# Second MoE: expert rests of 129 to 160 rows as one single block and one small block

## The chip, the cores and the metric

The kernel runs on one core of one Trainium2 chip. The metric is device time in microseconds (us) of one execution, the median of several; lower is better. Engines are named as in the profile: PE (TensorE), DVE (VectorE), ACT (ScalarE), POOL (GpSimd) and SP (SyncE, here only an issuer of DMAs).

## The reference, cut to what matters

Three stages run one after the other: a gated linear attention over 4 x 768 tokens with 8 heads of 48, a first MoE in which every token goes through all weights, and a second MoE in which every token goes to one of eight experts. Only the second MoE is changed:

```python
expert_idx = np.argmax(logits, axis=1)          # N = 3072 tokens, E = 8 experts
out = np.zeros((N, D), dtype=np.float32)        # D = 384
for e in range(E):
    mask = expert_idx == e
    h = np.maximum(x[mask] @ w1[e], 0.0)        # 384 x 1024
    out[mask] = gate_w[mask, None] * (h @ w2[e])  # 1024 x 384
```

On the inputs of the reference the eight experts get 1305, 521, 427, 153, 107, 15, 14 and 530 rows; of the first 22 of 24 tiles of 128 tokens they get 1199, 473, 380, 147, 98, 15, 14 and 490.

## The kernel before

**Stages.** Phase 1 computes attention and the first MoE; its instructions are recorded and put in an order by a planner of the kernel's own (all of them have line L368). Phase 2 is the second MoE. Between them, tokens are sorted into blocks of up to 128 rows: `route_early` does it for the first 22 tiles and hands out up to PE = 4 pairs of blocks (256 rows of one expert each); `late_route` does it for all rows that are left, on DVE, while phase 2 is already at work on the early blocks. It makes late pairs (up to PL = 8) of rests over 128 rows (`pairs_of` with `least` 129), single blocks of at most 128 rows, and up to MINI = 5 small blocks of at most MT = 32 rows. Its results are `btab` (expert of each step, and whether it differs from the step before), `mtab` (expert of each small block), `srcrow` (rows to gather), `dstrow` (rows to scatter to) and `slotgate`.

**Steps.** `STEPS` lists the blocks in order: block 0, block 1, then pairs (p) and single blocks (s). Before it is "ppppp" "s" "pppppp" behind the first two, so 14 steps, numbered k = 0 to 13; the blocks of pairs have the numbers 2 to 23, the single block 24. Further single blocks stand as spares and are run only if more are needed, which these inputs don't. Small blocks have no step: `WITH` names the steps beside which they run (5, 7, 9, 11, 12).

**A step** (`moe2`, driven by `phase2`): `load` fetches the expert's two weight matrices (1536 KB each, queues `q1_buf` and `q2_buf`, two sets deep) on SP's queue, with a condition: nothing is moved if the expert is that of the step before. `gather` fetches rows with an indirect DMA on POOL's queue into `xg`, two steps ahead, four buffers. `prep` splits the weights of the next step into a high and a low part: ACT writes `w1s` and `w2h` (L1288, L1297), DVE writes `w1l` and `w2l` (L1292, L1298); a single block needs no `w1l`. `transpose` turns the next step's rows on PE (`pxg`, L1313), ACT and DVE write `xh`, `xl`. `mm1` (L1336) writes `ph` in PSUM, three buffers; ACT takes `hhi` from it (L1340), DVE `hlo` (L1341). `mm2` (L1352) writes `py`, two buffers; ACT scales it to `yo` (L1356) and POOL scatters `yo` to `out` with an indirect DMA (L1358).

**A small block** (`small`) goes through seven stages between the parts of its step and the next one: load of `w1m` (L1371), gather of `xgm` (L1373), load of `w2m` (L1379), transposes `pxm` (L1383) with `xm` on ACT, matmul `phm` (L1390) with `hm` on ACT, transposes `pt` (L1397) with `hT` on DVE, matmul `pym` (L1405) with `part` on ACT, and one matmul `psm` (L1410) with `ym` on ACT. `w1m` and `w2m` have one buffer each, so the load of the next small block's `w1m` waits on SP for this one's `phm`, and `w2m` for `pym`.

**Order.** In phase 2 each engine's instructions are put in a fixed order when the program is built, by a scheduler that estimates times; then each engine, and each of the queues of SP and POOL, works strictly in that order. Every scatter to `out` also waits for the landing of the scatter before it. Two pieces decide which step carries a small block and when its first weights are asked for:

```python
                elif after:
                    load(k + 1)
                    p = prep(*STEPS[k + 1])
                if k in WITH:
                    next(small_now)                  # w2m
                if k + 1 in WITH:
                    small = self.small(pool, mp, pg, WITH.index(k + 1))
                    next(small)                      # w1m, xgm
                next(p, 0)
```

Of the kernel before, what the change touches and what calls it, by code (L numbers as in the profile page):

```python
# [15 lines left out]
ALU = mybir.AluOpType  # L16
# [11 lines left out]
E = 8  # L28
# [6 lines left out]

TE, PE, PL, SG = 22, 4, 8, E
KE, KP = 2 * PE, 2 * (PE + PL)
NBLK = KP + SG  # L40
MT, MINI = 32, 5

SPARE = 7


def steps(order):

    out, p, s = [(0, 1), (1, 1)], 2, KP
    for c in order:
        out.append((p, 2) if c == "p" else (s, 1))  # L50
        p, s = (p + 2, s) if c == "p" else (p, s + 1)
    assert (p, s) == (KP, NBLK - SPARE)
    return out + [(i, 1) for i in range(s, NBLK)]


STEPS = steps("ppppp" "s" "pppppp")

WITH = 5, 7, 9, 11, 12
NE, NS = 1 + PE, len(STEPS)

TESTS = 6 * NU + 6 + NTILE
# [46 lines left out]
def bc(ap, axis, n):  # L108

    a = ap.unsqueeze(axis)  # L110
    shape = list(a.shape)
    shape[axis] = n
    return a.to_broadcast(shape)
# [269 lines left out]
class Prog:  # L383
# [65 lines left out]
    def consts2(self):  # L449
# [7 lines left out]
        q.gpsimd.memset(self.order, -1.0)  # L457
        for k, (i, n) in enumerate(STEPS[NE:]):
            q.gpsimd.memset(self.order[:, k, 2 - n:3 - n], float((i - KE) // 2 if n == 2 else i - KP))
# [495 lines left out]
    def pairs_of(self, new, cnt, T, n, least, name):  # L955

        v = self.q.vector

        k256 = self.k128[:, 1 + (least == 256):min(T + 1, NTILE):2]
        gt, num, tk = new([E, k256.shape[1]], name + "gt"), new([E], name + "n"), new([E], name + "t")  # L960
        v.tensor_tensor(gt, bc(cnt, 2, k256.shape[1]), bc(k256, 1, E), op=ALU.is_ge if least == 256 else ALU.is_gt)
        v.tensor_reduce(num, gt, axis=AX.X, op=ALU.add)
        st, end = self.sums(new, num, name)
        v.tensor_scalar_min(tk, st, float(n))
        v.scalar_tensor_tensor(tk, end, float(n), tk, op0=ALU.min, op1=ALU.subtract)
        return num, st, end, tk
# [190 lines left out]
    def late_route(self, pool, pg):  # L1157

        v, t = self.q.vector, self.q.tensor
        T, N = NTILE, NBLK + MINI - KE  # L1160

        def new(shape, name, dt=F32):
            return pool.tile([128] + shape, dt, name=name)
        late = slice(TE, T)
        lg, mx = self.choose(new, self.ss[:, late], self.lg[:, late], self.oh[:, :, late])
        rank, cnt = self.ranks(new, pg.tile([128, 2, E, T], F32, tag="rt", bufs=1, name="within"), T)

        taken, slot = new([E], "taken256"), new([E, T], "slot1")

        def take(n):  # L1170
            v.tensor_scalar_mul(taken, n, 256.0)
            v.tensor_sub(cnt, cnt, taken)
            v.tensor_sub(rank, rank, bc(taken, 2, T))
        take(self.taken)
        left, base, ends = new([E, T], "left"), new([2, E], "base"), new([2, E], "ends")
        v.tensor_scalar(left, rank, 0.0, None, op0=ALU.is_ge)
        _, st, end, tk = self.pairs_of(new, cnt, T, PL, 129, "mid")
        v.tensor_copy(ends[:, 0], end)
        take(tk)

        v.tensor_add(base[:, 0], st, tk)
        v.tensor_scalar(base[:, 0], base[:, 0], 256.0, 1.0, op0=ALU.mult, op1=ALU.add)
        v.tensor_add(slot, rank, bc(base[:, 0], 2, T))
        v.scalar_tensor_tensor(slot, rank, 0.0, slot, op0=ALU.is_lt, op1=ALU.mult)

        gt, nb = new([E, T], "cgt"), new([E], "nblocks")
        v.tensor_tensor(gt, bc(cnt, 2, T), bc(self.k128, 1, E), op=ALU.is_gt)
        v.tensor_reduce(nb, gt, axis=AX.X, op=ALU.add)

        few, bm = new([E], "few"), new([MINI, E], "bem")  # L1190
        v.tensor_scalar(few, cnt, float(MT), None, op0=ALU.is_le)
        v.tensor_mul(few, few, nb)
        stm, endm = self.sums(new, few, "few")
        v.scalar_tensor_tensor(few, stm, float(MINI), few, op0=ALU.is_lt, op1=ALU.mult)
        v.tensor_sub(nb, nb, few)
        v.memset(endm[:, E - 1:], 4096.0)
        v.tensor_tensor(bm, bc(self.blk[:, :MINI], 2, E), bc(endm, 1, MINI), op=ALU.is_ge)
        em = new([MINI], "emini")
        v.tensor_reduce(em, bm, axis=AX.X, op=ALU.add)
        v.tensor_copy(self.mtab, em)  # L1200
        st, end = self.sums(new, nb, "late")
        v.tensor_copy(ends[:, 1], end)

        v.tensor_scalar(self.flags[:, 1:2], end[:, E - 1:], float(SG - SPARE), None, op0=ALU.is_gt)

        v.memset(ends[:, :, E - 1:], 4096.0)
        be, m = new([NS - NE, 2, E], "beq"), NS - NE
        v.tensor_tensor(be, bc(self.order, 3, E), bc(ends, 1, m), op=ALU.is_ge)
        v.tensor_reduce(self.bef[:, NE:], be, axis=AX.XY, op=ALU.add)
        v.tensor_copy(self.tab[:, 0, NE:], self.bef[:, NE:])  # L1210
        v.tensor_tensor(self.tab[:, 1, NE:], self.bef[:, NE:], self.bef[:, NE - 1:NS - 1], op=ALU.not_equal)

        v.tensor_scalar(base[:, 1], st, 128.0, 1.0 + 128 * (KP - KE), op0=ALU.mult, op1=ALU.add)

        v.tensor_scalar(stm, stm, 128.0, 1.0 + 128 * (NBLK - KE), op0=ALU.mult, op1=ALU.add)
        v.tensor_sub(stm, stm, base[:, 1])
        v.tensor_mul(stm, stm, few)
        v.tensor_add(base[:, 1], base[:, 1], stm)
        s2 = new([E, T], "slot2")
        v.tensor_add(s2, rank, bc(base[:, 1], 2, T))  # L1220
        v.scalar_tensor_tensor(s2, rank, 0.0, s2, op0=ALU.is_ge, op1=ALU.mult)
        v.tensor_add(slot, slot, s2)
        v.tensor_mul(slot, slot, left)
        self.gate(new, lg, mx, self.gates[:, late])
        yield
        at, val = self.slots(new, slot, T, N)
        ps = pg.tile([128, 5 * N], F32, tag="rt", bufs=1, name="slots")
        for t0 in range(0, T, 6):
            pos = pool.tile([128, 6, 128], BF16, tag="ohpos", bufs=2, name=f"ohpos{t0}")
            v.tensor_tensor(pos, bc(self.pos128, 1, 6), bc(at[:, t0:t0 + 6], 2, 128), op=ALU.is_equal)  # L1230
            self.place(ps, pos, val, t0)
        tok, e0 = new([N], "tok"), new([2, N], "empty")
        self.join(tok, self.gate_of[:, KE:], ps)
        v.tensor_scalar(e0[:, 0], tok, 1.0, 0.0, op0=ALU.subtract, op1=ALU.max)
        v.tensor_copy(self.src[:, KE:], e0[:, 0])
        v.tensor_scalar(e0[:, 1], tok, 0.0, 4097.0, op0=ALU.is_equal, op1=ALU.mult)
        v.scalar_tensor_tensor(e0[:, 1], tok, -1.0, e0[:, 1], op0=ALU.add, op1=ALU.add)
        v.tensor_copy(self.dst, e0[:, 1])
        self.flag(self.cp, pg)
        yield  # L1240
# [177 lines left out]
    def phase2(self):  # L1418
        tc, nc = self.tc, self.nc
        with ExitStack() as ctx:  # L1420
# [12 lines left out]
            late = self.late_route(rp, pg)  # L1433
            gather(*STEPS[1])
            load(0)
            first = prep(*STEPS[0])
            for _ in range(2):
                next(first)
            last = NS - SPARE
            few = iter(())  # L1440
            for k, (i, n) in enumerate(STEPS[:last]):
                if k + 2 < last:
                    gather(*STEPS[k + 2])
                p, after = iter(()), k + 1 < last
# [4 lines left out]
# [4 lines that stand above are left out]
                    next(small_now)  # L1453
                if k + 1 in WITH:

                    small = self.small(pool, mp, pg, WITH.index(k + 1))
                    next(small)
# [6 lines left out]
                for _ in few:  # L1464
                    pass
                if k in WITH:
                    few = small_now
                    next(few)
                if k + 1 in WITH:
                    small_now = small  # L1470
# [79 lines left out]
    def last_blocks(self):  # L1550

        nc = self.nc
        t, v, s, k0, i0 = nc.tensor, nc.vector, nc.scalar, NS - SPARE, STEPS[NS - SPARE][0]
        with self.tc.tile_pool(name="lb", bufs=1) as p, self.tc.tile_pool(name="lbg", bufs=1, space=PSUM) as pg, \
                self.tc.For_i(0, SPARE, 1) as k:

# [230 lines left out]
```

## Time and profile before

| | us |
|---|---|
| Median of 3 runs | 777.73 |
| Lowest and highest run | 777.09, 779.57 |
| The profiled execution | 777.83 |
| Its span in the trace | 775.9 |
| Phase 2, from its first `mm1` on PE to the end of the last `mm2` | 514.2 to 768.0 |

The profiled execution took 1.9 us more than the span of its trace. Times in the trace count from the span's start. In the trace the duration of one matmul overlaps with that of the next, so the length of a stretch of work on PE is taken from the start of its first matmul to the start of the next stretch. A step of phase 2 starts on PE with its first `ph` matmul and ends with the first of the next step.

### The profile page before, as it was taken

The page shows a single profiled execution, that of the slowest core. Times are in us where ns is not written, and L with a number is a line of the kernel's source. Part 1 is how long each engine was busy: PE and PEld are TensorE (multiplying, and loading weights), DVE is VectorE, ACT ScalarE, POOL GpSimd, SP SyncE. Part 2 cuts the span into 40 slices and gives each one's busy share as a digit, 9 for nine tenths or more (in the row PEclk, how much of TensorE's full clock was granted, in tenths as well). Part 3 has the DMA queues.
Part 4 walks back from the last instruction along what each step waited for, and adds up shares of the span by engine and source line. Part 5 has one row for each costly group of instructions (what it writes and reads, how often), then busy time and mean ns, then how long its engine had stood idle before and what let it go on. Part 6 is the DMA issues. An engine that isn't in the chain of part 4 may idle for free. (4 is left out here: it accounts for less than half of the span.)

```text
span 775.9 us, 18425 instructions
## 1 busy us (share of the span) xinstructions
PE 719.6 (93%) x7318; PEld 657.1 (85%) x7318; DVE 607.1 (78%) x1211; ACT 441.5 (57%) x1007; POOL 104.6 (13%) x156
## 2 busy tenths in 40 slices
PE   0568989999999999999999999999999999999995
PEld 0447679899899989888998988989989898999985
DVE  8999799999999999999999722869986455546420
ACT  8997485656667555757455442167535466544521
POOL 6301000000000000000000000022122223324211
PEclk9987899999999999999999999999999999999999
DMA  8608062635345380834516240051058775691500
GB/s 330 263 21 197 1 174 69 139 131 137 106 105 119 91 209 13 197 99 119 137 37 140 60 86 22 13 233 42 22 236 335 283 299 213 210 368 49 186 22 26
DMA packets 28753, 107.42 MB, mean 138 GB/s; under 512 B 5061, under 2 KB 8180, under 8 KB 25569
## 3 DMA queue, kind: packets, MB, share of 16 engines
q1 hardware_dynamic: 20432, 77.55, 33.5%
q0 software_dynamic: 7952, 28.21, 11.3%
q8 instruction: 59, 0.97, 0.5%
q10 hardware_dynamic: 272, 0.39, 0.1%
q14 instruction: 38, 0.30, 0.1%
HBM read 96.35 MB, written 10.62 MB: 138 GB/s over the span
## 5 line engine op out<-in xcount | busy, mean ns | idle before, releaser
L368 PE MATMUL ph<-xhi,w 128*128 128x256 f32 x864 | 134.0, 291 | 0.9 <-ACT xhi L368 0.9
L368 PEld LDWEIGHTS ph<-xhi,w 128*128 128x128 f32 x864 | 114.3, 191 | 8.3 <-issue 4.7
L1298 DVE TENSOR_TENSOR w2l<-queue_q_buf,w2h 128x768 fp32r<-128x768 f32 x52 | 47.9, 954 | 39.1 <-ACT w2h L1297 39.0
L1336 PE MATMUL ph<-xh,w1s 128*128 128x256 f32 x264 | 77.0, 292 | 0.0
L368 PE MATMUL ph<-xlo,w 128*128 128x256 f32 x432 | 75.3, 283 | 0.4 <-DVE xlo L368 0.4
L1336 PE MATMUL ph<-xh,w1l 128*128 128x256 f32 x264 | 74.6, 283 | 0.0
L1336 PE MATMUL ph<-xl,w1s 128*128 128x256 f32 x264 | 74.6, 283 | 0.0
L1352 PE MATMUL py<-w2h,hlo 128*128 128x384 f32 x200 | 67.9, 340 | 1.8 <-DVE hlo L1341 1.8
L1352 PE MATMUL py<-w2h,hhi 128*128 128x384 f32 x200 | 69.1, 345 | 0.0
L1352 PE MATMUL py<-w2l,hhi 128*128 128x384 f32 x200 | 67.6, 338 | 0.0
L368 PEld LDWEIGHTS ph<-xlo,w 128*128 128x128 f32 x432 | 62.0, 191 | 0.6 <-DVE xlo L368 0.6
L368 POOL DMA_DIRECT2D v<-v x24 | 12.9, 538 | 365.4 <-PE py L368 364.5
L1341 DVE SCALAR_TENSOR_TENSOR hlo<-ph,hhi 128x512 fp32r<-128x512 f32 x50 | 34.3, 688 | 30.0 <-ACT hhi L1340 30.0
L1340 ACT ACTIVATE hhi<-ph 128x512 fp32r<-128x512 f32 x50 | 29.9, 598 | 49.0 <-PE ph L1336 48.8
L368 PE MATMUL pa<-S 112*128 112x128 f32 x384 | 51.7, 279 | 2.2 <-DVE at L368 1.7
L1336 PEld LDWEIGHTS ph<-xh,w1s 128*128 128x128 f32 x264 | 50.5, 191 | 3.8 <-issue 3.1
L368 PEld LDWEIGHTS pa<-S 112*128 112x128 f32 x384 | 48.2, 193 | 4.5 <-DVE at L368 2.9
L1297 ACT CAST w2h<-queue_q_buf 128x768 fp32r x52 | 40.8, 833 | 18.1 <-PE py L1352 16.7
L1336 PEld LDWEIGHTS ph<-xh,w1l 128*128 128x128 f32 x264 | 50.5, 191 | 0.5
L1336 PEld LDWEIGHTS ph<-xl,w1s 128*128 128x128 f32 x264 | 50.5, 191 | 0.0
L368 DVE TENSOR_TENSOR sa<-X 128x384 f32<-128x384 f32 x84 | 46.5, 554 | 0.7
L1292 DVE TENSOR_TENSOR w1l<-queue_q_buf,w1s 128x1536 fp32r<-128x1536 f32 x22 | 38.6, 1759 | 9.3 <-PE ph L1336 7.4
(399 smaller groups left out, 1809.1 us busy)
## 6 DMA issues: line engine op xcount, KB each, us to landing
queue_q_buf<-w SPq DMA_DIRECT2D x26, 1536.0 KB
S<-QK SPq DMA_DIRECT2D x46, 289.1 KB
X<-a SPq DMA_DIRECT2D x11, 768.0 KB
QKr<-qk SPq DMA_DIRECT2D x11, 768.0 KB
w1m<-w SPq DMA_DIRECT2D x5, 1536.0 KB
w2m<-w SPq DMA_DIRECT2D x5, 1536.0 KB
v<-v POOLq DMA_DIRECT2D x24, 224.0 KB, 3.6
r<-w POOLq DMA_DIRECT2D x12, 384.0 KB, 8.4
```

Source lines behind the costliest of these rows:

```text
L368: getattr(getattr(self.nc, c[0]), c[1])(*c[2], **c[3])
L1292: v.tensor_sub(wl[k], av.rearrange("p (a b) -> p a b", b=FF2)[:, :, c], w1[k].bitcast(F32))
L1297: s.copy(hi, b[:, c])
L1298: v.tensor_sub(lo, bv[:, c], hi.bitcast(F32))
L1336: t.matmul(ph[:, f], a, b, start=o == 0, stop=o == len(ops) - 1)
L1340: s.activation(hi, ph, AF.Relu).ins,
L1341: v.scalar_tensor_tensor(lo, ph, 0.0, hi.bitcast(F32), op0=ALU.max, op1=ALU.subtract).ins]
L1352: t.matmul(py, a[:, f, r], c[:, k % 4], start=o == 0, stop=o == 3 * KF - 1)
```

## The change

Rests of 129 to 160 rows (128 + MT) are no longer a pair of two blocks. They go as one single block of 128 rows and one small block with the other 1 to 32. On the reference's inputs this concerns one expert, number 3 with 153 rows. There are then 7 late pairs, 2 single blocks and 6 small blocks, in 14 steps as before: block 0, block 1, "ppppppsppspp". The blocks of pairs have the numbers 2 to 21, the single blocks 22 and 23. `WITH` becomes 5, 6, 7, 9, 10, 12. By experts, steps 6 to 13 were 1, 4 (single), 1, 2, 2, 3, 7, 7, and are now 1, 1, 3 (single), 2, 2, 4 (single), 7, 7.

```diff
-TE, PE, PL, SG = 22, 4, 8, E
+TE, PE, PL, SG = 22, 4, 7, E + 2
-MT, MINI = 32, 5
-
-SPARE = 7
+MT, MINI = 32, 6
+
+SPARE = 8
-STEPS = steps("ppppp" "s" "pppppp")
-
-WITH = 5, 7, 9, 11, 12
+STEPS = steps("ppppppsppspp")
+
+WITH = 5, 6, 7, 9, 10, 12
...
-        v.tensor_tensor(gt, bc(cnt, 2, k256.shape[1]), bc(k256, 1, E), op=ALU.is_ge if least == 256 else ALU.is_gt)
+        v.scalar_tensor_tensor(gt, bc(cnt, 2, k256.shape[1]), float(least % 128), bc(k256, 1, E), op0=ALU.subtract,
+                               op1=ALU.is_ge)
...
-        _, st, end, tk = self.pairs_of(new, cnt, T, PL, 129, "mid")
+        _, st, end, tk = self.pairs_of(new, cnt, T, PL, 128 + MT + 1, "mid")
...
-        v.tensor_scalar(few, cnt, float(MT), None, op0=ALU.is_le)
-        v.tensor_mul(few, few, nb)
+        v.scalar_tensor_tensor(few, nb, -128.0, cnt, op0=ALU.mult, op1=ALU.add)
+        v.tensor_scalar(few, few, float(MT - 128), None, op0=ALU.is_le)
+        v.scalar_tensor_tensor(few, nb, 1.0, few, op0=ALU.min, op1=ALU.mult)
...
+        v.tensor_scalar_mul(nb, nb, 128.0)
         v.tensor_sub(stm, stm, base[:, 1])
+        v.tensor_sub(stm, stm, nb)
         v.tensor_mul(stm, stm, few)
-        v.tensor_add(base[:, 1], base[:, 1], stm)
-        s2 = new([E, T], "slot2")
-        v.tensor_add(s2, rank, bc(base[:, 1], 2, T))
+        s2, s3 = new([E, T], "slot2"), new([E, T], "slot3")
+        v.tensor_tensor(s3, rank, bc(nb, 2, T), op=ALU.is_ge)
+        v.tensor_mul(s3, s3, bc(stm, 2, T))
+        v.tensor_add(s3, s3, bc(base[:, 1], 2, T))
+        v.tensor_add(s2, s3, rank)
```

The order of phase 1 stays as it was, but for one more memset on POOL near the start. In phase 2 the scheduler gives other orders. Three places are shown, with the line numbers of each program (L1267 to L1413 of before are L1273 to L1419 of the changed program).

SP's queue, from a small block's second weights to the weights of a single block. Before, this is block 24 (`w2m0` belongs to the small block of step 5):

```order
L1379 DMA w2m0_8052<-w22 128x3072
L1251 TENSOR_LOAD btab_95
L1255 TENSOR_LOAD btab_95
L1257 ISA
L1260 COMPARE_AND_BRANCH
L1261 ISA
L1261 DMA queue_6708_q1_buf<-w21 128x3072
L1262 ISA
L1262 DMA queue_6709_q2_buf<-w22 128x3072
```

In the changed program, the same for block 22 (`w2m1` and `w1m2` belong to the small blocks of steps 6 and 7):

```order
L1385 DMA w2m1_8360<-w22 128x3072
L1374 TENSOR_LOAD mtab_103
L1377 ISA
L1377 DMA w1m2_8365<-w21 128x3072
L1257 TENSOR_LOAD btab_95
L1261 TENSOR_LOAD btab_95
L1263 ISA
L1266 COMPARE_AND_BRANCH
L1267 ISA
L1267 DMA queue_6709_q1_buf<-w21 128x3072
L1268 ISA
L1268 DMA queue_6710_q2_buf<-w22 128x3072
```

The single block's weights now stand behind `w1m2`, the first weights of the next small block. The same holds for block 23, behind `w1m4`.

ACT, where the single block's `w1s` is copied from the queue. Before, this stands in the first matmuls of step 5 (blocks 8 and 9):

```order
L1340 ACTIVATE hhi8_0_1_8122<-ph8_0_1_8103 128x512
L1385 COPY xm0_8130<-pxm0_8126 128x96
L1274 ISA
L1288 COPY w1s24_0_8369<-queue_6708_q1_buf 128x1536
L1340 ACTIVATE hhi8_1_0_8153<-ph8_1_0_8134 128x512
L1340 ACTIVATE hhi8_1_1_8176<-ph8_1_1_8157 128x512
L1288 ISA
L1288 COPY w1s24_1_8370<-queue_6708_q1_buf 128x1536
```

In the changed program it stands in the second matmuls of step 6 (blocks 10 and 11), followed by `w2h` and the first `hhi` of step 7:

```order
L1362 ACTIVATE yo10_8562<-py10_0_8537,slotgate_102 128x384
L1294 COPY w1s22_0_8686<-queue_6709_q1_buf 128x1536
L1294 COPY w1s22_1_8687<-queue_6709_q1_buf 128x1536
L1362 ACTIVATE yo11_8599<-py10_1_8574,slotgate_102 128x384
L1413 COPY part1_8613<-pym1_8604 128x384
...
L1303 COPY w2h22_0_8688<-queue_6710_q2_buf 128x768
L1303 COPY w2h22_1_8690<-queue_6710_q2_buf 128x768
L1346 ACTIVATE hhi12_0_0_8712<-ph12_0_0_8693 128x512
```

The copies of the single block's weights moved from two steps ahead of its step to a step and a half ahead, and now have `yo11`, `part1` and `hhi12` behind them. Further on in step 7, the copy `w1s14_0` of the pair after it stands ahead of `hhi12_1_0`. Steps 9 and 10 have the same order with blocks 14, 23, 16 and 18 in place of 10, 22, 12 and 14.

POOL's queue, at the end of step 3 (blocks 4 and 5), where the gathers for step 5 (`xg8`, `xg9`) wait for `srcrow` of `late_route`. Before:

```order
L1358 DMA out<-yo3_7483,srcrow_97 3072x384
L1267 DMA xg8_7490<-x1d_113,srcrow_97 128x384
L1267 DMA xg9_7494<-x1d_113,srcrow_97 128x384
L1267 DMA xg10_7743<-x1d_113,srcrow_97 128x384
L1267 DMA xg11_7747<-x1d_113,srcrow_97 128x384
L1358 DMA out<-yo4_7704,srcrow_97 3072x384
L1358 DMA out<-yo5_7736,srcrow_97 3072x384
L1373 DMA xgm0_7799<-x1d_113,srcrow_97 128x384
```

In the changed program:

```order
L1364 DMA out<-yo3_7490,srcrow_97 3072x384
L1364 DMA out<-yo4_7711,srcrow_97 3072x384
L1364 DMA out<-yo5_7743,srcrow_97 3072x384
L1273 DMA xg8_7497<-x1d_113,srcrow_97 128x384
L1273 DMA xg9_7501<-x1d_113,srcrow_97 128x384
L1273 DMA xg10_7750<-x1d_113,srcrow_97 128x384
L1273 DMA xg11_7754<-x1d_113,srcrow_97 128x384
L1379 DMA xgm0_7806<-x1d_113,srcrow_97 128x384
```

Two scatters went ahead of the gathers, and the small block's gather no longer stands behind them. On DVE in the same place, the last `hlo` of step 3 (`hlo4_1_0`, `hlo4_1_1`) stood behind the large operations of `late_route` (`ohval`, `ohpos`), and now stands ahead of them; `xl6` and one `w2l8` now stand ahead of `srcrow`.

## Rows read from the trace of the kernel before

**Rows 1.** The page: the span, and PE's busy time.
```profile
span 775.9 us, 18425 instructions
PE 719.6 (93%) x7318; PEld 657.1 (85%) x7318; DVE 607.1 (78%) x1211; ACT 441.5 (57%) x1007; POOL 104.6 (13%) x156
```

**Rows 2.** Who PE waited for, 512 to 776 us.
```profile
PE py L1352 <- DVE hlo L1341: 1.8, 1, 1.8
PE pxm L1383 <- DMA xgm<-x1d,srcrow: 0.8, 1, 0.8
```

**Rows 3.** Stretches: steps 3, 4, 7, 9, 10, and a part of step 3.
```profile
core 0: us, PE busy (x) PEld busy (x) DVE busy (x) ACT busy (x) POOL busy (x), PEclk, DMA share, GB/s
552.93:576.66 23.73, 21.93 (x156) 21.07 (x155) 22.88 (x45) 10.08 (x14) 5.13 (x4) 0.93 0.28 110
576.66:594.05 17.39, 17.39 (x126) 17.39 (x126) 9.80 (x13) 9.98 (x14) 5.08 (x5) 1.00 1.01 412
634.38:646.80 12.42, 12.42 (x108) 11.35 (x108) 6.21 (x9) 8.70 (x13) 5.04 (x5) 1.00 0.45 162
666.76:688.20 21.44, 21.44 (x173) 19.09 (x172) 11.93 (x14) 11.77 (x19) 6.59 (x5) 1.00 0.69 250
688.20:706.56 18.36, 18.36 (x133) 18.09 (x129) 9.87 (x12) 9.66 (x15) 5.06 (x5) 1.00 0.62 246
...
572.00:576.00 4.00, 4.00 (x17) 4.00 (x16) 3.27 (x10) 0.36 (x1) 2.80 (x3) 0.58 1.00 421
```

**Rows 4.** PE in order of time, step 5: start, length, operation.
```profile
604.13 1.50 PE L1390 MATMUL phm<-w1m,xm 128*32 128x256 f32 x24
605.56 0.87 PE L1313 MATMUL pxg<-ident,xg 128*128 128x128 f32 x6
...
610.44 0.38 PE L1397 MATMUL pt<-ident,hm 128*128 128x128 f32 x2
...
614.94 1.50 PE L1405 MATMUL pym<-w2m,hT 128*32 128x384 f32 x16
```

**Rows 5.** SP's queue in order of time: two weight loads of step 5.
```profile
605.69 0.34 SPq L1371 DMA_DIRECT2D w1m<-w  x1
607.43 0.34 SPq L1261 DMA_DIRECT2D queue_q_buf<-w  x1
```

**Rows 6.** SP's DMA queue: packets and MB from 605.6 to 617.5, 622, 630 us.
```profile
q1 hardware_dynamic: 282, 3.18, 70.8%
...
q1 hardware_dynamic: 431, 4.82, 75.2%
...
q1 hardware_dynamic: 726, 8.02, 81.4%
```

**Rows 7.** Groups of ACT and DVE, 590 to 776 us: busy, mean ns | idle before.
```profile
L1297 ACT CAST w2h<-queue_q_buf 128x768 fp32r x32 | 25.1, 832 | 10.7 <-PE py L1352 10.7
...
L1288 ACT CAST w1s<-queue_q_buf 128x1536 fp32r x12 | 17.7, 1480 | 0.0
...
L1407 ACT COPY part<-pym 128x384 f32<-128x384 f32 x5 | 2.4, 478 | 1.7 <-PE pym L1405 1.7
...
L1298 DVE TENSOR_TENSOR w2l<-queue_q_buf,w2h 128x768 fp32r<-128x768 f32 x32 | 29.2, 955 | 35.4 <-ACT w2h L1297 35.4
L1292 DVE TENSOR_TENSOR w1l<-queue_q_buf,w1s 128x1536 fp32r<-128x1536 f32 x14 | 24.6, 1758 | 8.4 <-PE ph L1336 6.7 <-ACT w1s L1288 1.7
L1341 DVE SCALAR_TENSOR_TENSOR hlo<-ph,hhi 128x512 fp32r<-128x512 f32 x34 | 23.4, 688 | 29.5 <-ACT hhi L1340 29.4
```

**Rows 8.** Late routing in order of time, on DVE and POOL.
```profile
551.90 0.36 DVE L1220 TENSOR_TENSOR slot<-incl,base 128x192 f32<-128x192 f32 x1
...
571.63 0.17 DVE L1235 CAST srcrow<-empty 128x29 int32<-128x29 f32 x1
...
572.59 1.04 POOL L1267 DMA_INDIRECT xg<-x1d,srcrow  x1 [16.83 <-issue]
```

**Rows 9.** Landing after issue: gathers for step 5; then the scatter at 578.2.
```profile
DMA to landing us min/median/max: 7.1/7.5/7.9
...
DMA to landing us min/median/max: 11.1/11.1/11.1
```

## The prediction

> **What bounds the kernel now.** First I read the page's busy times: PE works 93% of the span [rows 1]. Only phase 2 changes its order, so next I read who PE waited for in phase 2. Two waits are worth naming: 1.8 us on DVE's `hlo` and 0.8 us on the gather `xgm0` [rows 2]. Then I cut phase 2 into its steps [rows 3]: in steps 4, 7, 9 and 10 PE is busy for the whole stretch. So the time of phase 2 is the sum of what its steps cost on PE, plus stalls, and the change can do two things: alter that sum, and move waits to where PE has to stop. Both need a price.
>
> **What a step costs on PE.** Four stretches give it [rows 3]. A plain pair (step 4) takes 17.39 us. A pair with a small block (step 9) takes 21.44 us, so the small block's four larger pieces cost 21.44 − 17.39 = 4.05 us. A pair that starts with the last piece of the small block before it, `psm` (step 10), takes 18.36 us, so `psm` costs 0.97 us. Step 7, the single block with all pieces of a small block but `pym` and `psm`, takes 12.42 us. How much of that is the single block can be read in two ways. By the price in a pair, the small block's share is 4.05 less `pym` (some 1.43, the 1.50 of [rows 4] less its overlap), and 9.80 is left. By the pieces themselves it is `phm`, 1.43 (from 604.13 to the next start at 605.56 [rows 4]), and about 0.4 of transposes, and 10.5 is left. Both hold six transposes for the next pair; a step in front of a single block needs three, 0.4 us less (six take 0.87 us [rows 4]).
>
> **Term 1, the work saved.** One pair (17.39) goes; a single block (9.80 to 10.5) and a small block (4.05 + 0.97 = 5.02) come, and 0.4 us of transposes goes: between −3.0 and −2.3, I take **−2.7 us**, since one small block also moves from a single block's step to a pair's. The work left is bound by PE, so it counts in full. In bytes nothing changes: the late steps load seven different sets of weights and the small blocks five before, six and six now, as expert 1's two late pairs stand side by side.
>
> **Term 2, `xgm0`.** POOL's queue had the scatters of `yo4` and `yo5` ahead of the gather `xgm0`. Now they stand ahead of `xg8`, and `xgm0` follows `xg11` directly. It is asked for several us earlier, and the wait of 0.8 us [rows 2] goes: **−0.8 us**. If something else is late there by as much, 0.
>
> **Term 3, steps 3 to 5, where late routing is done.** Step 3 takes 23.73 us against 17.39 for a plain pair; with the transposes and the low clock near its end (0.58 granted in 572 to 576, 0.93 over the step [rows 3]) some 4 us of it are lost. PE waits there for `hlo`, which stands on DVE behind the large operations of late routing; DVE is busy 22.88 of 23.73 us [rows 3]. The changed order puts that `hlo` first, so step 3 gets shorter. But the same DVE time now lies ahead of `srcrow`, which ended at 571.63 + 0.17 [rows 8]: one `hlo` (0.69), one `w2l` (0.96) [rows 7], two `xl` (0.5 each, as an `hlo` of 384 in place of 512 columns) and the new routing arithmetic (three operations of up to 0.36 on 192 columns, by the row of `slot` [rows 8], and some short ones) come ahead: about 3.2 to 3.6 us, `srcrow` at 574.8. POOL then issues `xg8` at 575.8 (1.0 behind, as 572.59 was [rows 8]) and `xg9` 1.3 later; they land 7.1 to 7.9 us after issue [rows 9], the second at 585.0. PE, 3.5 us ahead of before, wants them at about 581.4 and stops. What was gained in step 3 is given back in front of step 5, all but **−0.5 us**. Bounds: −3.5 if the routing is as early as before, +1.5 if PE's clock drops after this stop as it did in 572 to 576, when PE came out of the wait on `hlo`.
>
> **Term 4, the weights of the two single blocks.** This is the term that decides. SP's queue works in order, and `w1m` and `w2m` have one buffer each. In the changed program expert 3's weights are queued behind `w1m2`, which waits for the end of `phm1` in step 6, and the weights of the pair after it behind `w2m2`, which waits for the end of `pym1`. Call the end of `phm1` T0. Step 5 of before has this same set of requests, so it serves as a clock: `phm` ends at 604.13 + 1.50 = 605.63 [rows 4], `w1m` is issued at 605.69 and the next expert's first matrix at 607.43 [rows 5]; `w2m` can go when `pym` ends, 614.94 + 1.50 [rows 4]. From 605.6 the queue has moved 3.18 MB by 617.5, 4.82 by 622 and 8.02 by 630 [rows 6]. A matrix is 1.57 MB, so the second (`w1` of the single block) is complete at about T0 + 12.4 with its completion, the third (`w2`) at T0 + 17, the fourth (`w2m`) at T0 + 21 and the fifth (`w1` of the next pair) at T0 + 25.
>
> Before, nobody stood at these landings: ACT's `w1s` copies had no idle time in front at all [rows 7], since the single block's weights were asked for two steps ahead and copied in the next step. Now ACT comes to `w1s22_0` right after `yo10`, at about T0 + 5.6, and waits 7 us. (Places on PE and ACT are counted from T0 by the order, with the lengths of rows 3, 4 and 7.) Behind it in ACT's order stand:
> - the second half of `w1s` (1.48 each), `yo11` and `part1` (about 0.5 each, `part` 0.48) [rows 7]: 12.4 + 2.96 + 1.1 = T0 + 16.6 for `part1`. PE needs it for `psm1`, which comes at T0 + 15.3 by the order of PE. Wait 1.3.
> - three `w2h` (0.83 each), DVE's `w2l` behind them (0.96) [rows 7], and then the first `hhi` and `hlo` of the single block: `hlo12_0_0` is done at T0 + 21.5. There are three `ph` buffers; PE wants the first one back, for its fourth `ph`, at T0 + 19.7. With the wait above counted in, 1.8 more.
> - `w1s14_0` stands ahead of `hhi12_1_0` and needs the fifth load, T0 + 25: copied 26.5, `w1l` behind it on DVE (1.76 [rows 7]) 28.2, `hlo12_1_0` (0.69) 28.9. PE wants that buffer at T0 + 27.6. Wait 1.2.
>
> That is 1.3 + 1.8 + 1.2 = 4.3 us, and steps 9 and 10 have the same queue and the same order around block 23: twice, **+8.6 us**. Bounds: 0, if the loads land early enough (the first rival), and 12 if after the stops of each place PE runs 4 us at 0.58 as in 572 to 576 [rows 3] (0.42 x 4 = 1.7 us per place).
>
> **At nothing:** the memset on POOL in phase 1, which is 13% busy [rows 1]; the last steps, which end in a pair with a `psm` as before; the sixth small block's ACT and DVE work, which lies beside PE's.
>
> **The sum.** −2.7 − 0.8 − 0.5 + 8.6 = +4.6. The profiled execution took 777.83 (775.9 of span and 1.9 around it), 0.1 from the median. 777.8 + 4.6 = **782.4 us**.
>
> **Rivals.** *The loads are in time (faster).* Between 572 and 576 the DMA engines moved 421 GB/s with weights all but alone [rows 3]. At that rate 3.15 MB take 7.5 us and `w1` of expert 3 is there at T0 + 8.5; `w1s` is done at 11.4, `part1` at 12.5 (wanted 15.3), and the fifth load at T0 + 19.7 lets `hlo12_1_0` end at 23.7, ahead of PE. Then term 4 is 0 and the time 777.8 − 4.0 = 773.8. It decides at a landing of about T0 + 11, where `part1` is just in time. Against it: with the same requests the queue moved only 3.18 MB by 617.5 [rows 6], as three gathers and a scatter run at the same time, and these are there in the changed program too (`xgm2`, `xg14`, `xg15`, the scatter of `yo10`). Chance 0.18.
>
> The Trainium skill, page "DMA: Bandwidth & Descriptors", section "Where 436 GB/s comes from", says that transfers between HBM and SBUF are held to some 358 GB/s by the HBM side, and that 435 is the limit of the fabric. The 421 of rows 3 speaks against the lower figure and agrees with the higher. By the lower figure, as an estimate, two matrices take 8.8 us and the stops would be small, so this page speaks for the faster side.
>
> *Half of it.* With the second landing at T0 + 11 (between 8.5 and 12.4) the first stop vanishes and the others shrink to about 2.3 us per place: 777.8 − 4.0 + 4.6 = 778.4. Chance 0.18.
>
> *The scatters get in front of the gathers (slower).* Every scatter waits for the landing of the one before, and that took up to 11.1 us [rows 9]. `yo4` and `yo5` now stand ahead of `xg8`. If `yo4` takes the 11.1 rather than the 7 or so that I let pass, `xg8` and `xg9` land 3.8 later and PE stops that much longer in front of step 5: 782.4 + 3.8 = 786.2. It decides where `yo5` is issued later than `srcrow` is there. Chance 0.10.
>
> *The change does not do what it says.* If expert 3 still went as a pair, seven late pairs would not hold all rows and a spare would run; by the counts (153 = 128 + 25) it does not. Chance 0.02, priced as no change or worse.
>
> **How the numbers follow.** Forecast 0.52, the rivals as above. 0.3% (2.3 us) is about what a measurement of this kernel can tell from no change. Faster than 775.4: the first rival, **0.18**. Within: the half case, **0.19**. Slower than 780.1: forecast, third rival and the rest, **0.63**. The range leaves out the first rival and little else: from 775.5, below the half case, to 788, which takes in the third rival and some 2 us of clock: 775.5 to 788.
>
> **What will show it.** Right, if ACT waits for a DMA ahead of `w1s22` and `w1s23`, where it never did before, and PE for ACT's `part` and DVE's `hlo` in steps 7 and 10; if a plain pair is still 17.39 us and the two single steps are near 10.5, one `psm` more where there is one; if the wait on `xgm0` is gone and one on `xg8` or `xg9` stands in its place; if step 3 is near 20 us. Wrong, if these `w1s` copies have no idle time in front, if expert 3's `w1` lands by T0 + 9, or if PE's clock is below 1.00 in stretches after a stop, which I did not price in the forecast.

## The result and the profile after

| | before | changed |
|---|---|---|
| Median | 777.96 (5 runs) | 786.98 (5 runs) |
| Lowest and highest run | 777.09, 779.57 | 784.68, 789.29 |
| The profiled execution, its span | 777.83, 775.9 | 789.29, 787.3 |

The changed kernel is slower: the ratio is 1.0113, with a 95% interval of 1.0083 to 1.0143. The prediction said 782.4, between 775.5 and 788. Direction and range held by the median, though two of the five runs lie above 788, and the loss is 9.0 us where 4.6 was forecast. The profiled execution of the changed kernel is the longest of its five, 2.3 us above the median, so what follows adds up to 11.5 us and not to 9.0.

The page, span and busy times, to be read against [rows 1]:

```profile
span 787.3 us, 18407 instructions
PE 721.2 (92%) x7314; PEld 652.7 (83%) x7314; DVE 602.0 (76%) x1211; ACT 440.6 (56%) x1007; POOL 101.3 (13%) x157
```

Who PE waited for in phase 2 (us in total, times, longest), the view of [rows 2], without the first wait of the stage, which both kernels have, and waits of 0.6 us and less. A wait of PE is called a stop from here on.

```profile
PE pxg L1319 <- DMA xg<-x1d,srcrow: 4.4, 2, 3.0
PE py L1358 <- DVE hlo L1347: 2.6, 2, 1.3
PE ph L1342 <- DVE hlo L1347: 1.8, 2, 0.9
PE psm L1416 <- ACT part L1413: 1.4, 2, 0.7
```

The two waits of [rows 2] are gone, and four kinds came in their place: one in front of step 5 (in two parts, 3.0 and 1.4), and three that each occur twice, once in step 7 and once in step 10.

Steps of the changed kernel as stretches, the view of [rows 3]: step 3, step 4, the end of step 4 (behind its stop), steps 6, 7, 8 and 10, a part of step 10, and step 11:

```profile
core 0: us, PE busy (x) PEld busy (x) DVE busy (x) ACT busy (x) POOL busy (x), PEclk, DMA share, GB/s
553.73:573.19 19.46, 19.08 (x145) 18.54 (x145) 19.39 (x30) 10.21 (x15) 1.96 (x2) 1.00 0.06 21
573.19:599.41 26.22, 21.84 (x138) 21.19 (x136) 14.32 (x31) 10.16 (x14) 9.27 (x8) 0.87 0.77 301
588.44:599.41 10.97, 10.97 (x50) 10.97 (x49) 1.57 (x3) 5.38 (x6) 2.02 (x2) 0.75 0.64 248
620.86:643.05 22.19, 22.19 (x178) 19.43 (x174) 10.93 (x13) 8.23 (x15) 6.29 (x6) 1.00 0.70 256
643.05:668.67 25.62, 22.71 (x175) 19.13 (x171) 11.64 (x13) 16.21 (x24) 5.92 (x6) 1.00 0.82 343
668.67:679.62 10.95, 10.95 (x85) 10.69 (x82) 5.16 (x8) 7.89 (x12) 3.63 (x4) 1.00 0.51 178
701.06:728.57 27.51, 24.51 (x175) 20.63 (x171) 11.64 (x13) 16.20 (x24) 5.89 (x6) 0.94 0.77 320
719.24:727.21 7.97, 7.97 (x40) 7.62 (x44) 3.81 (x5) 2.70 (x5) 1.00 (x1) 0.79 0.35 140
728.57:739.52 10.95, 10.95 (x85) 10.69 (x82) 5.16 (x8) 7.90 (x12) 2.61 (x3) 1.00 0.42 154
```

Read against before, step 3 got shorter, 19.46 for 23.73, and step 4 longer, 26.22 for 17.39. Together they are 45.68 for 41.12: 4.6 us lost. Part of what step 3 gained is work that moved into step 4: some of late routing's matmuls run there now (step 3 has 11 matmul records fewer, step 4 has 12 more). Steps 7 and 10 hold the same work as step 6 but for three transposes (0.3 us less): 21.9 us. They take 25.6 and 27.5, so 3.7 and 5.6 us are lost there. The single steps, 8 and 11, take 10.95 each, with a `psm` at the start.

The whole: 0.8 up to the start of step 3 (late at 553.73 for 552.93), 4.6 in steps 3 and 4, 5.4 from step 5 to the end of the last `py`, and 0.7 behind it and outside the span: 11.5 us.

**Where steps 7 and 10 lose it.** SP's queue, the loads around the end of `phm1` (632.31, the T0 of the prediction), the view of [rows 5]:

```profile
632.37 0.34 SPq L1377 DMA_DIRECT2D w1m<-w  x1
634.02 0.34 SPq L1267 DMA_DIRECT2D queue_q_buf<-w  x1
634.70 0.34 SPq L1268 DMA_DIRECT2D queue_q_buf<-w  x1
643.18 0.33 SPq L1385 DMA_DIRECT2D w2m<-w  x1
644.88 0.34 SPq L1267 DMA_DIRECT2D queue_q_buf<-w  x1
```

ACT in order of time (start, length, operation, idle time before it and what ended it), steps 6 and 7:

```profile
644.60 2.85 ACT L1294 COPY w1s<-queue_q_buf 128x1536 f32 x2 [6.65 <-DMA queue_q_buf<-w]
647.35 0.57 ACT L1362 ACTIVATE yo<-py,slotgate 128x384 f32<-128x384 f32 x1
647.83 0.47 ACT L1413 COPY part<-pym 128x384 f32<-128x384 f32 x1
648.56 2.30 ACT L1303 CAST w2h<-queue_q_buf 128x768 fp32r x3 [0.27 <-DMA queue_q_buf<-w]
...
656.96 1.48 ACT L1294 CAST w1s<-queue_q_buf 128x1536 fp32r x1 [3.77 <-DMA queue_q_buf<-w]
```

The single block's `w1` is complete 12.3 us after T0, as forecast, and ACT stands for 6.65 us with `part` behind it. The next pair's `w1` (656.96) is complete 24.6 after T0.

**Where steps 3 to 5 lose it.** DVE: `srcrow` (before at 571.63 [rows 8]):

```profile
576.10 0.17 DVE L1241 CAST srcrow<-empty 128x30 int32<-128x30 f32 x1
```

SP's queue at the same time:

```profile
574.36 0.35 SPq L1377 DMA_DIRECT2D w1m<-w  x1
576.11 0.35 SPq L1267 DMA_DIRECT2D queue_q_buf<-w  x1
576.79 0.34 SPq L1268 DMA_DIRECT2D queue_q_buf<-w  x1
577.34 0.33 SPq L1385 DMA_DIRECT2D w2m<-w  x1
```

The landing of `xg8` and `xg9`, issued at 577.06 and 578.72, after their issue (the view of [rows 9]):

```profile
DMA to landing us min/median/max: 8.9/9.0/9.1
```

Four matrices, 6.3 MB, are asked for within 3 us, just when the gathers are issued on which PE waits.

### The profile page after: what moved, and what is told of

It reads as the page before. It is cut to its first block, busy times and chain, and to the rows that moved or that the text cites. A ratio compares the mean times of both kernels' runs of the same rounds, so it can differ in the third digit from the quotient of the medians.

```text
span 787.3 us, 18407 instructions
## 1 busy us (share of the span) xinstructions
PE 721.2 (92%) x7314; PEld 652.7 (83%) x7314; DVE 602.0 (76%) x1211; ACT 440.6 (56%) x1007; POOL 101.3 (13%) x157
## 5 line engine op out<-in xcount | busy, mean ns | idle before, releaser
L1342 PE MATMUL ph<-xh,w1s 128*128 128x256 f32 x240 | 69.7, 291 | 1.8 <-DVE hlo L1347 1.8
L1358 PE MATMUL py<-w2h,hlo 128*128 128x384 f32 x192 | 66.2, 345 | 2.6 <-DVE hlo L1347 2.6
L1342 PE MATMUL ph<-xh,w1l 128*128 128x256 f32 x240 | 67.8, 283 | 0.0
L1342 PE MATMUL ph<-xl,w1s 128*128 128x256 f32 x240 | 67.6, 283 | 0.0
L1347 DVE SCALAR_TENSOR_TENSOR hlo<-ph,hhi 128x512 fp32r<-128x512 f32 x48 | 32.6, 685 | 25.7 <-ACT hhi L1346 25.7
L1342 PEld LDWEIGHTS ph<-xh,w1s 128*128 128x128 f32 x240 | 45.8, 191 | 5.0 <-issue 2.5
L1342 PEld LDWEIGHTS ph<-xh,w1l 128*128 128x128 f32 x240 | 45.9, 191 | 0.1
L1342 PEld LDWEIGHTS ph<-xl,w1s 128*128 128x128 f32 x240 | 45.8, 191 | 0.2 <-DVE xl L1325 0.2
L368 DVE TENSOR_TENSOR m<-X,C 128x768 f32<-128x768 f32 x48 | 44.3, 950 | 1.8 <-ACT C L368 1.7
```

What stands on the lines that cost most here:

```text
L368: getattr(getattr(self.nc, c[0]), c[1])(*c[2], **c[3])
L1342: t.matmul(ph[:, f], a, b, start=o == 0, stop=o == len(ops) - 1)
L1347: v.scalar_tensor_tensor(lo, ph, 0.0, hi.bitcast(F32), op0=ALU.max, op1=ALU.subtract).ins]
L1358: t.matmul(py, a[:, f, r], c[:, k % 4], start=o == 0, stop=o == 3 * KF - 1)
```

## The experiments

Two theories came out of this. **Queue:** in steps 7 and 10 the loss comes from SP's order, since ACT stands at a copy whose load waits behind `w1m`. **Late routing:** in steps 3 to 5 it comes from the added arithmetic, which turns the order on DVE. Their common rival is that the new split costs more in itself. Each edit below is against the changed kernel, but for the one that says otherwise; `...` marks lines left out.

### The arithmetic alone

The new arithmetic, with the old bound and the old blocks.

```diff
-TE, PE, PL, SG = 22, 4, 7, E + 2
+TE, PE, PL, SG = 22, 4, 8, E
...
-MT, MINI = 32, 6
+MT, MINI = 32, 5
-SPARE = 8
+SPARE = 7
...
-STEPS = steps("ppppppsppspp")
+STEPS = steps("ppppp" "s" "pppppp")
-WITH = 5, 6, 7, 9, 10, 12
+WITH = 5, 7, 9, 11, 12
...
-        _, st, end, tk = self.pairs_of(new, cnt, T, PL, 128 + MT + 1, "mid")
+        _, st, end, tk = self.pairs_of(new, cnt, T, PL, 129, "mid")
```

> The kernel before with the late routing's new arithmetic alone (bound 129 kept, so the same blocks, 8 late pairs, 1 single, 5 small ones). Theory (late routing): the added operations on DVE turn the order around hlo4 and srcrow, srcrow comes about 4 us later, xg8 and xg9 land late and PE stops in front of step 5, then runs at a lower clock: steps 3 and 4 together 45 to 46 us where before had 41.1, the wait on xgm0 gone, total 777.96 + 4.6 - 0.8 = about 781.8. Rival (it is the new layout, its sixth small block or the scatters, not the arithmetic): only the operations themselves, at most 1.1 us, 778 to 779.

Measured: 781.32 against 778.44, ratio 1.0035 (1.0021 to 1.005), 2.9 us where 3.4 to 3.8 were expected. PE's waits in phase 2, and steps 3 and 4:

```profile
PE pxg L1319 <- DMA xg<-x1d,srcrow: 4.9, 2, 4.0
```
```profile
553.25:572.25 19.00, 19.00 (x146) 18.53 (x145) 18.92 (x30) 10.07 (x14) 4.66 (x2) 1.00 0.05 19
572.25:598.53 26.28, 21.34 (x136) 20.69 (x136) 14.04 (x31) 10.28 (x14) 9.87 (x8) 0.87 0.95 370
```

Steps 3 and 4 are 45.3 us, as in the changed kernel (45.7), and the stop is much the same (4.9 us for 4.4). The late routing's arithmetic does this without any new block.

### One collision with the old blocks

The kernel before, with one small block moved so that the single block's weights come to stand behind `w1m1`.

```diff
-WITH = 5, 7, 9, 11, 12
+WITH = 5, 6, 9, 11, 12
```

> The kernel before with the small blocks beside steps 5, 6, 9, 11, 12 in place of 5, 7, 9, 11, 12: old arithmetic, old blocks, but the single block's weights now stand behind w1m1, which waits for phm0, as in the changed kernel. Theory (queue): ACT waits 6 to 7 us for the DMA ahead of w1s24, PE stops for part0, hlo10_0_0 and hlo10_1_0, 2.9 us in the gaps and 0.6 more around them: 777.96 + 3.5 = 781.5, up to 1 more where the clock drops. Rival (the single and small blocks cost more in themselves, and the queue is hidden): no work is added, so 778.

Measured: 782.02 against 778.44, ratio 1.0047 (1.0031 to 1.0063): 3.6 us for 3.5. ACT's waits for weights from 590 us on, where before had none at `w1s` [rows 7], PE's stop in step 6 (624.74), and four us behind it as a stretch (columns as above):

```profile
ACT w1s L1288 <- DMA queue_q_buf<-w: 9.6, 2, 6.0
```
```profile
PE ph L1336 <- DVE hlo L1341: 1.8, 1, 1.8
```
```profile
626.00:630.00 4.00, 4.00 (x34) 2.62 (x33) 0.15 (x1) 1.27 (x1) 1.01 (x1) 0.59 1.02 428
```

No block, no matmul and no byte was added; one small block moved one step earlier, so that the single block's loads stand behind `w1m1`. The size came out as expected, its parts did not: of the three stops expected (2.9 us) one of 1.8 is there, and behind it the granted clock fell to 0.59 for 4 us, which costs about 1.6. The wait on `xgm0` is gone in this trace too, so the 3.6 is net of it: steps 6 to 8 of the trace are 4.0 us longer than before. So a place by itself costs 4.0 us (in the trace) to 4.4 (the 3.6 and the 0.8), and the changed kernel has two.

### Other steps for the small blocks

```diff
-WITH = 5, 6, 7, 9, 10, 12
+WITH = 5, 6, 8, 9, 11, 12
```

> The changed kernel with the small blocks beside steps 5, 6, 8, 9, 11, 12 in place of 5, 6, 7, 9, 10, 12, so that the weights of each single block no longer stand behind a w1m that waits for the phm of the step before last. Theory (queue): the stops of steps 7 and 10 go, 7.0 us with what lies around them, and the clock that followed, 1 to 2: 786.98 - 7.0 - 1 = about 779; the loss in steps 3 and 4 stays (45 to 46 us). Rival (the blocks themselves cost it): 787 as before this edit, with the stops elsewhere.

Measured: 783.81, ratio 1.0071 (1.0053 to 1.0089), about 3.2 below the changed kernel where 8 were expected. The three stops of steps 7 and 10 are gone, and another stands in step 9. PE's waits above 0.5 us, but for the first of the stage, then ACT's row ahead of that stop:

```profile
PE pxg L1319 <- DMA xg<-x1d,srcrow: 5.1, 2, 4.0
PE pt L1403 <- DVE xl L1325: 3.2, 1, 3.2
```
```profile
692.07 1.47 ACT L1294 COPY w1s<-queue_q_buf 128x1536 f32 x1 [6.20 <-DMA queue_q_buf<-w]
```

Expert 4's weights now stand behind `w2m3` (issued at 679.86, the end of `pym2`), and ACT again waits until 12.2 us after that. Behind the copy stood `xh`, and so PE's transposes. The mechanism is the expected one; what I missed is that the new table makes the same collision one step further on. So this run confirms the cause but gave back only part of the time.

### Two of the operations on POOL

```diff
+        g = self.nc.gpsimd
         v.tensor_tensor(s3, rank, bc(nb, 2, T), op=ALU.is_ge)
-        v.tensor_mul(s3, s3, bc(stm, 2, T))
-        v.tensor_add(s3, s3, bc(base[:, 1], 2, T))
+        g.tensor_tensor(s3, s3, bc(stm, 2, T), op=ALU.mult)
+        g.tensor_tensor(s3, s3, bc(base[:, 1], 2, T), op=ALU.add)
```

> The changed kernel with two of the new operations on 192 columns (the product and the sum of slot3) on POOL in place of DVE, which lets the order put srcrow ahead of xl6 and w2l8 again. Theory (late routing): srcrow comes some 3 us earlier, the stop in front of step 5 shrinks from 4.4 to 1.5 us or less and the low clock behind it goes: 786.98 - 4.6 - 0.5 = about 782; the stops in steps 7 and 10 stay. Rival (the layout, not the arithmetic): 787.

Measured: 783.90, ratio 1.0068 (1.0052 to 1.0084), 3.1 to 3.5 below the changed kernel where 5 were expected. Steps 3 and 4:

```profile
553.84:575.71 21.87, 20.76 (x158) 19.71 (x157) 21.30 (x41) 10.07 (x14) 1.78 (x3) 1.00 0.13 42
575.71:594.42 18.71, 17.63 (x123) 17.19 (x123) 12.21 (x19) 10.07 (x14) 9.41 (x8) 1.00 0.95 384
```

They are 40.6 us for 45.7: the stop shrank from 4.4 to 0.8 and the low clock went, all of the 5 expected. The rest of the profiled run, the slowest of its six, was longer than in the changed kernel, with one more stop of 1.4 us in step 10. The stops of step 7 stayed, as expected.

### The small block's first weights asked for later

Only SP's order is to change: `w1m` goes with `w2m`, behind the weights of the next step.

```diff
-        w1 = mp.tile([128, KD, FF2], F32, tag="w1m", bufs=1, name=f"w1m{m}")
-        nc.sync.dma_start(w1, self.io["w21"][bass.ds(e, 1)].rearrange("a p (k f) -> p (a k) f", f=FF2))
         xg = pool.tile([128, DM], F32, tag="xg", bufs=4, name=f"xgm{m}")
...
         yield
 
+        w1 = mp.tile([128, KD, FF2], F32, tag="w1m", bufs=1, name=f"w1m{m}")
+        nc.sync.dma_start(w1, self.io["w21"][bass.ds(e, 1)].rearrange("a p (k f) -> p (a k) f", f=FF2))
         w2 = mp.tile([128, KF, DM], F32, tag="w2m", bufs=1, name=f"w2m{m}")
```

> The changed kernel with one edit: a small block's w1m is asked for a step later in the program, together with its w2m, so that on SP the weights of expert 3 and of expert 4 stand ahead of w1m2 and w1m4 and behind w2m1 and w2m3, which wait for the end of pym a step earlier: 9 to 10 us earlier than now. Blocks, steps and arithmetic stay. Theory (queue): the three stops of steps 7 and 10 (7.0 us with what is around them) and the low clock behind the second shrink to at most one stop of about 1.3 us per place: 786.98 - 6.5 = about 780.5 (779 to 782); steps 3 and 4 stay at 45 to 46 us. Rival (the blocks cost it): no change, 787.

Measured: 783.56, ratio 1.0062 (1.0042 to 1.0083), outside the expected 779 to 782. PE's waits from step 3 on, but for two of 0.4 and less:

```profile
PE pxg L1319 <- DMA xg<-x1d,srcrow: 4.1, 1, 4.1
PE py L1358 <- DVE hlo L1347: 2.5, 3, 1.3
PE py L1358 <- ACT hhi L1346: 0.8, 1, 0.8
```

In steps 6 and 7 two stops of 0.5 and 0.7 are left of the 2.9 that step 7 had, but in step 10 two of 0.8 and 1.3 remain. ACT's row ahead of these:

```profile
711.07 1.48 ACT L1294 CAST w1s<-queue_q_buf 128x1536 fp32r x1 [6.63 <-DMA queue_q_buf<-w]
```

These are the weights of expert 7, behind `w2m4` (issued at 698.42, when `pym3` ended): complete 12.6 us after it. The expectation looked at experts 3 and 4 alone. Steps 3 and 4 stayed at 45.1, as expected. But the step's own matrices go out at 564.9 there, and only `w1m0` and `w2m0` (573.97 and 576.20) meet the gathers. Two matrices in place of four, and the landing of `xg8` and `xg9` (issued at 577.13 and 578.49) is as late as with four:

```profile
DMA to landing us min/median/max: 8.7/9.1/9.5
```

Together with the POOL edit:

> Both cures at once: slot3's product and sum on POOL, and w1m asked for with w2m. Theory: the two losses are independent, so this gives w1late less what the POOL edit gave (3.1 to 3.5): about 777 (775 to 779); if no stop were left in steps 6 to 11, 777.96 - 2.7 - 0.8 - 0.5 = 774. Rival (one loss hides the other, or a saved stop comes back as another wait): 780 or more.

Measured: 781.95, ratio 1.0038 (1.0023 to 1.0053). That is 1.6 to 1.9 below `w1late`, not 3.1 to 3.5, and the expected 775 to 779 was missed; the case of no stop at all was not reached, since four at `hlo` (3.4 us) were left in the profiled run, the slowest of its nine.

### No small block beside step 5

```diff
-WITH = 5, 6, 7, 9, 10, 12
+WITH = 6, 7, 8, 10, 11, 12
```

> The changed kernel with the small blocks beside steps 6, 7, 8, 10, 11, 12, so that no small block's weights are asked for at the moment late routing ends. Question: why xg8 and xg9 took 8.9 and 9.1 us to land where before had 7.1 and 7.9. Theory (the burst of w1m0, the step's two matrices and w2m0, 6.3 MB, issued within 3 us of the gathers): with two matrices in place of four, xg8 and xg9 land in 7 us or less and the stop in front of step 5 shrinks from 4.4 to about 2.5. Rival (the two scatters ahead of them on POOL's queue): these stay, so 8.9 and 9.1 stay. The total is not the question here, since the later weights meet ACT in other places: 780 to 788.

Measured: 785.15 in all, ratio 1.0099 (1.0074 to 1.0124). The question was the landing. SP's queue, the landing of `xg8` and `xg9` (issued at 577.1 and 578.4), and steps 3 and 4:

```profile
564.54 0.35 SPq L1267 DMA_DIRECT2D queue_q_buf<-w  x1
565.25 0.35 SPq L1268 DMA_DIRECT2D queue_q_buf<-w  x1
573.62 0.33 SPq L1377 DMA_DIRECT2D w1m<-w  x1
```
```profile
DMA to landing us min/median/max: 4.8/5.2/5.6
```
```profile
552.99:573.01 20.02, 19.63 (x149) 19.04 (x149) 19.95 (x31) 10.76 (x16) 1.94 (x2) 1.00 0.41 150
573.01:591.96 18.95, 18.45 (x133) 17.85 (x131) 13.61 (x30) 9.57 (x13) 9.03 (x8) 1.00 0.78 279
```

`w1m0` is issued within 0.05 us of the end of the last `slots` matmul of late routing, here as in the kernels before and after the change (the program opens its memory only when that of late routing is closed). With a small block beside step 5, the step's own matrices stand behind it and all four come at once. Without one, the step's own go out 9 us ahead of it, and only `w1m0` meets the gathers. The same two scatters stand ahead of the gathers here as in the changed kernel. The landing falls from 9.0 to 5.2, the stop from 4.4 to 0.5, and the clock stays at 1.00. `w1late` is the closest comparison: its second scatter (575.85 for 575.81) and its gather `xg8` (577.13 for 577.09) go out at the same times, and what differs beside the gathers is the second matrix, `w2m0`; there the landing is 9.1. So it is the weights. My expectation had counted two matrices and 7 us or less; with two, as `w1late` shows, nothing is gained. Steps 3 and 4 take 39.0 us together, 2.1 less than before the change, with the same added arithmetic as in the changed kernel: that arithmetic costs its 4.6 us only where the gathers meet the weights. The total stays high: this table brings three stops at `psm` (7.1 us in sum) and one at `ph` (1.9).

### Both causes cured

Two edits: `w1m` with `w2m`, and another table.

```diff
-WITH = 5, 6, 7, 9, 10, 12
+WITH = 6, 7, 8, 10, 11, 12
```

> w1late (w1m asked for with w2m) with the small blocks beside steps 6, 7, 8, 10, 11, 12, so that neither the gathers for step 5 meet a small block's weights nor the single blocks' weights stand behind a pym that ends less than a step earlier. Theory (burst and queue, both cured): steps 3 and 4 together 39 us (before 41.1), no stop in front of step 5 above 0.5, one stop of 0.7 in step 7 for the weights of expert 2, saved work 2.7 and no wait on xgm: 778.4 - 2.1 - 2.7 - 0.8 + 0.7 = about 773.5 (772 to 776), faster than the kernel before. Rival (what is saved comes back as another wait, as it did in wB and wE): 778 to 784, with a stop of 2 us or more in steps 6 to 12.

Measured: **772.26** against 778.62, ratio 0.9922 (0.9906 to 0.9938): faster than both kernels. PE's waits in phase 2, all of them but those of 0.4 and less and the first of the stage, and steps 3 and 4:

```profile
PE py L1358 <- DVE hlo L1347: 0.6, 1, 0.6
PE within L937 <- DVE oneh L914: 0.6, 1, 0.6
```
```profile
553.03:573.05 20.02, 19.64 (x149) 19.05 (x148) 19.95 (x31) 10.76 (x16) 1.95 (x2) 1.00 0.40 151
573.05:591.46 18.41, 18.28 (x132) 17.87 (x131) 13.56 (x30) 9.46 (x13) 9.78 (x8) 1.00 0.57 196
```

Here no weights at all move while the gathers for step 5 run, and these land after 3.8 to 4.4 us. A neighbouring table, with the same late `w1m`:

```diff
-WITH = 6, 7, 8, 10, 11, 12
+WITH = 6, 8, 9, 10, 11, 12
```

> As f1 with the small blocks beside steps 6, 8, 9, 10, 11, 12. Theory: as f1 in steps 3 and 4; expert 3's and 2's weights wait for nothing, but expert 4's stand behind w2m2 (end of pym in step 8) and expert 7's behind w2m3 (end of pym in step 9), each copied by ACT some 8 to 10 us later: one stop of 0.7 to 1.3 us in step 9 and in step 10: about 774.5 (773 to 777). Rival: as for f1.

Measured: 777.30, ratio 0.9984 (0.9969 to 1.0), just outside the expected 773 to 777: in step 9 stands one stop of 3.3 us (PE's `pt` behind DVE's `xl`, as in `wB`) where I expected about 1, and in step 10 one of 1.1.

### What the other split is worth

As the kernel with both causes cured, but with the old blocks.

```diff
-TE, PE, PL, SG = 22, 4, 7, E + 2
+TE, PE, PL, SG = 22, 4, 8, E
...
-MT, MINI = 32, 6
+MT, MINI = 32, 5
-SPARE = 8
+SPARE = 7
...
-STEPS = steps("ppppppsppspp")
+STEPS = steps("ppppp" "s" "pppppp")
-WITH = 6, 7, 8, 10, 11, 12
+WITH = 6, 8, 9, 11, 12
...
-        _, st, end, tk = self.pairs_of(new, cnt, T, PL, 128 + MT + 1, "mid")
+        _, st, end, tk = self.pairs_of(new, cnt, T, PL, 129, "mid")
```

> The blocks of the kernel before (8 late pairs, 1 single, 5 small ones; bound 129) with everything else as in f1: the new arithmetic of late routing, w1m asked for with w2m, the small blocks from step 6 on (6, 8, 9, 11, 12). Question: what the other split of expert 3 is worth once nothing stops PE. Theory (term 1, saved work): f1 is 2.3 to 3.0 faster, so 772.3 + 2.7 = 775 (0.996 of the kernel before), up to 1 more for a stop at the weights of expert 3 in step 9. Rival (the cures gave all of it): 772 to 773.

Measured: 775.34 against 777.87, ratio 0.9959 (0.9943 to 0.9976). The new split is 3.1 us faster (2.9 by the two ratios) when next to nothing stops PE in either: from step 3 on the stops are 1.0 us in sum with the new blocks and 0.6 with the old ones. The two intervals do not overlap, so the sign is shown; the size is known to some 2 us, since the kernels were measured in two series and each ratio has about 1.2 us of interval to either side. So of the 6.4 us that the cured kernel gains, about 3 are the change's own and the rest is that of the cures, which the old blocks profit from as well.

## Why the prediction was right, and where its sizes were off

**Term 1, −2.7: right.** In the profile it is 5.4 (steps 5 to 13) + 0.8 (the wait on `xgm0`, gone) − 9.3 (lost in steps 7 and 10) = −3.1; by the last experiment −2.9 to −3.1, give or take 2. That is the end of the bounds that came from the prices in a pair (9.80 for the single block).

**Term 2, −0.8: right.** No wait on an `xgm` is left.

**Term 4, +8.6: right in mechanism and place, and in its sum partly by luck.** The landing came 12.3 us after T0 for 12.4, ACT stood 6.65 us for 7, the fifth load was there at 24.6 for 25, and PE stopped for `part`, for `hlo` in the `ph` and behind the next pair's `w1s`, twice. The stops themselves are shorter (0.73, 0.89 and 1.29 us in step 7, 2.9 for 4.3), but each leaves some 0.3 us around it, and in step 10 the clock fell: 0.94 over the step, 0.79 from 719 to 727. The sum is 3.7 + 5.6 = 9.3: stops a third shorter than forecast, made up for by two costs that the forecast had at nothing. `b56` shows the cause with one small block moved and nothing added.

**Term 3, −0.5: wrong, it is the step that failed.** It measured +4.6 in steps 3 and 4. Its first half held: step 3 is 4.3 shorter, and `srcrow` comes 3.7 later against the start of the step. I used 3.2 there; the terms that I named add up to 3.7. The step that failed is that the gain of step 3 would be given back in front of step 5 and no more: step 4 got 8.8 us longer. Of these, 4.4 are the stop. I took the gathers' landing from [rows 9], 7.1 to 7.9, and they took 8.9 and 9.1, so the stop ended at 587.9, 587.1 without the 0.8 by which the whole trace was late, where I had 585.0. Then 2.5 are the clock, which I left out of the forecast and bounded at +1.5 with the rest: behind the stop PE ran at 0.75 on the mean of 11 us, and the 48 `py` matmuls took 10.97 us where step 4 of before needs 8.43. The prediction did say that the clock would prove it wrong. The last 1.9 lie in front of the first `py`: late routing's matmuls that moved over from step 3, and transposes that the stop split; I had both at nothing, and how they share it was not taken apart. The row that would have warned me is the burst on SP's queue: `wE` shows that the four matrices and the gathers go out together because `w1m0` waits for late routing. Why the gathers take 7.5 us to land before and 9.0 after, with the same four requests, is not settled. The two scatters ahead neither make it late by themselves (`wE` has them and lands at 4.8 and 5.6) nor are they needed for it: in `poolw1late`, with four matrices and no scatter in the 19 us ahead of `xg8`, the landings are 7.5 and 9.5.

**The rivals.** The loads were not in time: 12.3 us after T0, not 8.5 or 11. From 632 to 645 us the DMA engines moved 4.53 MB, 348 GB/s on the mean of 13 us, and only 0.20 MB from 632.3 to 634.3, which the first rival had left out. The Trainium skill, page "DMA: Bandwidth & Descriptors", section "Where 436 GB/s comes from", puts the limit of transfers between HBM and SBUF at about 358 GB/s; the stretch of 421 [rows 3] shows more, and the estimate of 8.8 us that I drew from the page was short of the 12.3 measured: it has neither the slow start nor the gathers that share the engines. The third rival, scatters in front of the gathers, had the right place (a longer stop in front of step 5), but `wE` and `w1late` show another cause, the weights. The upper end of the range, 788, had taken in its 3.8 us and some 2 us of clock. Of these only the clock came, so that the range held is in part luck.

**The sum by experiment.** 2.9 (arithmetic alone, with the gain on `xgm0` in it) + two places − 3.0 (saved work). The gain on `xgm0` must not count again in the places, so each is 4.0 (steps 6 to 8 of `b56`) to 4.4 (3.6 + 0.8), and the sum is 7.9 to 8.7, against 9.0 measured by the medians. What is left is smaller than what the intervals leave open (1.1 to 2.3 us to either side of each difference).

## What to carry to other kernels

On a queue that works in order, as SP's here, a transfer is as late as the request ahead of it that waits longest, and the price shows up on the engine that copies it and in whatever stands behind the copy, not at the queue. Moving a block from one step to another moves such meetings too: of the four runs with another table on the new blocks, three made a stop of 3 us or more somewhere else (`wB`, `wE`, `f2`), so every first request behind a wait has to be compared with the place of its copy. And when an edit shifts the moment at which two bursts are released, look up what else is in flight at that time before taking a landing from another place, and bound what the clock can lose behind a stop.

## What the runs showed of the hardware

The time from issue to landing of the gathers behind `srcrow` depended on the weights that were asked for beside them, but not in proportion: 3.2 to 4.4 us with none (`f1`, `f2`), 4.8 to 5.6 with one matrix of 1.57 MB (`wE`), 8.7 to 9.5 with two (`w1late`), 7.1 to 9.5 with four (before, the changed kernel, `poolw1late`).

After a stop the granted clock fell in some places and not in others: behind the 4.4 us in front of step 5 it was 0.75 on the mean of 11 us (a mix of the levels of 1.2 and 2.4 GHz), behind the three shorter stops of step 7 it stayed at 1.00, behind the same three in step 10 it was 0.79, and behind the one of 1.8 us in `b56` it was 0.59 for 4 us. So the length of a stop did not settle it here, and what did was not tried. The five runs of the changed kernel spread over 4.6 us; those of before over 2.5 in the series beside them, and over 5.3 in the 17 runs beside the last experiment.
